# Attention paced by the projections and moved further ahead, the last two heads turned by the tensor engine, and one weight load held back, in a fused attention and MLP block

## The chip, the cores and the metric

The kernel runs on one core of a Trainium2 chip. The metric is the time of one execution on the device, in microseconds (us). A difference counts as faster or slower when it is over 2% and clear of the noise.

TensorE is the matrix engine (PE in the profile), VectorE is DVE, ScalarE is ACT, GpSimd is POOL, and SyncE is SP. The last one only issues DMA transfers here. Below, to turn a matrix is to transpose it, and SBUF is the core's own memory.

## The reference, cut to what matters

```python
# x: (1, 2048, 1024); Wq, Wk, Wv: (1024, 32, 128); Wo: (32, 128, 1024)
# attention in 64 segments of 32 tokens, each with 8 memory tokens in front
def attention(x, mem0, Wq, Wk, Wv, Wo, seg_len):
    for s in range(n_seg):
        h = concat([mem, x[segment s]])
        q, k, v = h @ Wq, h @ Wk, h @ Wv              # 32 heads
        p = softmax(where(mask, q @ k.T * scale, -1e9))
        o = sum over heads of (p @ v) @ Wo
        mem = o[:, :8]; outs.append(o[:, 8:])
...
x = x + ga * attention(layernorm(x) * (1 + ca) + sa, ...)
x = x + gb * mixer_mlp(layernorm(x) * (1 + cb) + sb)  # first product: @ w1
```

The kernel guesses the memory tokens, checks the guess at the end, and so treats all segments at once: 22 tiles of about 99 rows for each head. Most of the projections are computed by a fast matrix product, with seven block products in place of eight; its matmuls are 480 columns wide, and a last part of 199 columns is multiplied in the ordinary way.

## The kernel before: the parts that matter

Three stages matter: the **projections** (Q, K and V of a pair of heads, with the attention of the pair before woven in), the **handover**, and the **Wo blocks** (four blocks of 512 tokens, each over all 32 heads). Then comes the stage that reads `w1s`. The Wo tile (n2, hc) is half n2 of the columns of Wo for group hc of eight heads. In the code below an empty list and the flip of the memory rows, which goes by a small DMA transpose `MT<-O`, are left out.

```python
def attention():                       # the attention as lists of small units, one list a pair
    per_hp = {}; waiting = []
    for h in range(H):
        lst = per_hp.setdefault(h // 2, [])
        for g in range(5):
            lst.append(lambda h=h, g=g: scores(h, g))
            while waiting and waiting[0][0] <= 5 * h + g - 1:
                lst.append(waiting.pop(0)[1])
            for j in range(8):
                if VG[j][-1] // 5 == g:
                    waiting.append((5 * h + g, lambda h=h, j=j: outs(h, j)))
                    if j == 7:
                        waiting.append((5 * h + g, lambda h=h: flip(h)))      # O -> OT by DMA transpose
                        waiting.append((5 * h + g + 3, lambda h=h: keep(h)))  # OT -> OTx_d in memory
                        if h % 2 and h + 2 < H:
                            waiting.append((5 * h + g + 2, lambda h=h: to_v(h + 2)))  # VT -> V by DMA
    per_hp["end"] = [u for _, u in waiting]
...
for hp in range(NHP - 1):              # projections of pair hp + 1, attention of pair hp
    fill = P_units(hp + 1)
    ...
    interleave(att[hp], fill)          # an attention unit, then its share of the projection units
...                                    # --- handover ---
W0, W0_load = W_units(0)               # Wo block 0, as [n2][hc][tt]
for j in range(1, 3):
    W0_load(0, j, nc.gpsimd)           # Wo tile (0, j), 1 MB, into one of 4 wstream buffers
    load_ot(j, nc.gpsimd)              # OTc j: the turned outputs of 8 heads, 1 MB, from OTx_d
for t, src in RW:                      # four rows, broadcast: 1.5 MB
    nc.gpsimd.dma_start(t[:], src.partition_broadcast(P))
load_wo2(NHP - 2)
interleave(att[NHP - 1], M_units(NHP - 3) + [lambda: load_wo2(NHP - 1)] + W0[0][0] + W0[0][1] + M_units(NHP - 2))
for u in att["end"] + W0[0][2]:
    u()
for j in range(3, 6):
    load_ot(j)
...
for us in W0[1][0:3] + W0[0][3:] + W0[1][3:]:   # heads 24..31 (hc = 3) last
    for u in us:
        u()
...
for blk in range(1, 4):
    ...
    else:                              # before block 3, in the program's order
        nc.sync.dma_start(w1s[:], B_w1.rearrange("(k p) n -> p k n", p=P))   # 2 MB
```

The order of each engine's instructions is set by a scheduler when the kernel is built: work that is ready early is moved ahead. So `w1s`, written before block 3, is issued in block 0. The `SyncE` queue is then worked off in order.

## Time and profile before

Median 1517.26 us of four runs (1515.22 to 1517.58); the profiled execution spans 1517.1 us.

I read the length of each stage from the timeline of TensorE. The projections run from the first fast-product matmul (at 122 us) to the end of the last one over 199 columns; the handover ends with the first matmul of Wo block 1, so it holds the last two heads and block 0; the blocks end with the first matmul that reads `w1s`.

| stage | us before | what TensorE waits for in it |
|---|---|---|
| start | 122.1 | not touched |
| projections with attention | 661.1 | some 12 us in all |
| handover, block 0 | 90.2 | 24.4 us, and half clock |
| Wo blocks 1 to 3 | 169.6 | under 1 us, but half clock at its start |
| rest | 474.0 | not touched |

TensorE's waits by line and releaser, before. The columns are the us in total, how often, and the longest:

```profile
PE ps_o L713 <- DMA V<-VT: 15.0, 2, 13.6
...
PE acc L845 <- DMA wstream<-in_A_Wo_dram: 7.2, 1, 7.2
...
PE acc L607 <- ACT snap L575: 3.8, 14, 0.5
PE acc L845 <- DMA OTc<-OTx_d: 3.6, 2, 1.8
PE acc L328 <- DVE KT L579: 3.3, 2, 1.7
...
PE acc L607 <- DVE VT L579: 1.6, 3, 1.1
```

L713 is the outputs of the attention, L845 the Wo blocks, L607 and L328 the projections. The first, second and fourth lines belong to the handover, apart from 1.5 us for V at the very start. The timeline of TensorE shows where they sit; each line has start, length, instructions, and in brackets the idle time before it and what ended it:

```profile
796.03 1.90 PE L845 MATMUL acc<-wstream,OTc 128*128 128x512 bf16 x8 [1.83 <-DMA OTc<-OTx_d]
...
815.64 0.86 PE L713 MATMUL ps_o<-V,E 104*104 104x129 bf16 x6 [13.56 <-DMA V<-VT]
...
850.96 2.76 PE L845 MATMUL acc<-wstream,OTc 128*128 128x512 bf16 x12 [1.77 <-DMA OTc<-OTx_d]
...
873.45 31.89 PE L845 MATMUL acc<-wstream,OTc 128*128 128x512 bf16 x134 [7.24 <-DMA wstream<-in_A_Wo_dram]
```

Why V of head 31 came so late is seen in the timeline of the SyncE queue, with start and time spent at issuing. The lines between are left out:

```profile
785.21 16.14 SPq L728 DMA_TRANSPOSE OT<-O  x1
...
803.66 5.33 SPq L650 DMA_TRANSPOSE V<-VT  x1
...
824.32 9.13 SPq L728 DMA_TRANSPOSE OT<-O  x1
...
849.82 0.84 SPq L978 DMA_DIRECT2D w1s<-in_B_w_dram  x1
```

Issuing the transpose of head 29 alone held the queue for 16 us, while 6.5 MB of the handover's loads, issued from 783.3 to 788.5 us, were in flight. V stood behind it. The last view is of stretches of five microseconds, with each engine's busy time, then the granted TensorE clock (1.00 is full), the busy share of the DMA engines, and GB/s:

```profile
810.00:815.00 5.00, 0.00 (x0) 0.00 (x0) 0.00 (x0) 0.00 (x0) 0.00 (x0) 0.50 1.08 237
815.00:820.00 5.00, 4.36 (x17) 2.32 (x18) 1.50 (x5) 0.88 (x3) 0.00 (x0) 0.50 0.98 236
...
870.00:875.00 5.00, 1.55 (x4) 0.59 (x5) 4.90 (x10) 1.93 (x5) 0.59 (x2) 0.50 1.07 372
875.00:880.00 5.00, 5.00 (x15) 1.89 (x14) 0.61 (x3) 0.00 (x0) 0.00 (x0) 0.59 1.09 383
```

After the two long waits TensorE worked at half clock for a while, and the DMA engines were full throughout.

### The profile page before, as it was taken

The page shows a single profiled execution, that of the slowest core. Times are in us where ns is not written, and L with a number is a line of the kernel's source. Part 1 is how long each engine was busy: PE and PEld are TensorE (multiplying, and loading weights), DVE is VectorE, ACT ScalarE, POOL GpSimd, SP SyncE. Part 2 cuts the span into 40 slices and gives each one's busy share as a digit, 9 for nine tenths or more (in the row PEclk, how much of TensorE's full clock was granted, in tenths as well). Part 3 has the DMA queues.
Part 4 walks back from the last instruction along what each step waited for, and adds up shares of the span by engine and source line. Part 5 has one row for each costly group of instructions (what it writes and reads, how often), then busy time and mean ns, then how long its engine had stood idle before and what let it go on. Part 6 is the DMA issues. An engine that isn't in the chain of part 4 may idle for free.

```text
span 1517.1 us, 24283 instructions
## 1 busy us (share of the span) xinstructions
PE 1429.2 (94%) x9074; PEld 760.1 (50%) x9074; DVE 921.4 (61%) x1961; ACT 668.2 (44%) x1403; POOL 356.1 (23%) x490
## 2 busy tenths in 40 slices
PE   5699999999999999999996799999997999999998
PEld 3365555556555655555653344444443444444443
DVE  5827777677676676766751343363287657675684
ACT  2715666665656665665650020122533661046400
POOL 7501100000000000000010222122011654535625
PEclk9999999999999999999998999999999999999999
DMA  9577779877778876778689999994299784377812
GB/s 307 193 279 158 154 163 197 169 161 158 152 163 197 169 171 153 154 159 193 131 220 292 323 328 327 290 270 146 64 276 270 231 265 157 100 246 240 281 52 77
DMA packets 406900, 304.81 MB, mean 201 GB/s; under 512 B 203370, under 2 KB 359018, under 8 KB 404850
## 3 DMA queue, kind: packets, MB, share of 16 engines
q1 hardware_dynamic: 367920, 239.39, 61.3%
q0 software_dynamic: 9616, 33.05, 7.3%
q10 hardware_dynamic: 29234, 30.71, 6.6%
q8 instruction: 73, 1.20, 0.3%
q14 instruction: 57, 0.47, 0.1%
HBM read 200.82 MB, written 50.63 MB: 166 GB/s over the span
## 4 chain that ended last, share of the span: by engine, by line
PE 73%; DMA 8%; issue 6%; DVE 5%; ACT 4%; POOL 3%; SPq 1%; ACTq 0%; DVEq 0%; POOLq 0%
PE acc L607 28%; PE bank_b L1202 6%; PE acc L845 6%; PE bank_b L1151 6%; PE acc L995 4%; PE acc L328 4%; PE bank_d L1151 3%; PE bank_d L1202 2%; PE bank_e L1202 2%; PE ps_o L713 2%; PE ps_s L698 2%; PE acc L318 2%; PE acc L1078 2%; PE bank_e L1151 1%; DVE ln_st L104 1%
## 5 line engine op out<-in xcount | busy, mean ns | idle before, releaser
L845 PE MATMUL acc<-wstream,OTc 128*128 128x512 bf16 x960 | 214.7, 385 | 11.3 <-DMA wstream<-in_A_Wo_dram 7.2
L607 PEld LDWEIGHTS <-T 128*128 128x128 f16 x1408 | 131.1, 97 | 123.2 <-issue 7.4
L575 ACT COPY snap<-acc 128x480 f32<-128x480 f32 x264 | 146.6, 564 | 101.9 <-PE acc L607 91.3
L607 PE MATMUL acc<-hs,T 128*128 128x480 f16 x704 | 158.5, 365 | 4.9 <-ACT snap L575 3.8
L607 PE MATMUL acc<-hh,T 128*128 128x480 bf16 (+1 forms) x704 | 162.3, 366 | 0.5 <-DVE VT L579 0.5
L845 PEld LDWEIGHTS <-OTc 128*128 128x128 bf16 x960 | 94.4, 99 | 124.8 <-DMA wstream<-in_A_Wo_dram 7.4
L740 POOL DMA_DIRECT2D OTx_d<-OT x32 | 24.8, 775 | 511.4 <-DMA OT<-O 495.2
L1151 PEld LDWEIGHTS <-ring 128*128 128x128 f16 (+1 forms) x784 | 77.5, 99 | 109.5 <-issue 17.6
L702 ACT ACTIVATE E<-ps_s 99x495 bf16<-99x495 f32 (+2 forms) x160 | 86.3, 543 | 65.0 <-PE ps_s L698 63.3
L607 PE MATMUL acc<-hh,wq 128*128 128x480 bf16 x464 | 105.3, 366 | 0.0
L579 DVE TENSOR_TENSOR KT<-acc,snap 128x480 bf16<-128x480 f32 x116 | 74.6, 655 | 47.0 <-PE acc L607 45.4
L720 DVE TENSOR_TENSOR O<-ps_o,rin_all 99x384 bf16<-99x384 f32 (+1 forms) x192 | 96.6, 510 | 3.8
L713 PE MATMUL ps_o<-V,E 99*99 99x129 bf16 (+2 forms) x704 | 81.1, 222 | 16.0 <-DMA V<-VT 15.0
L713 PEld LDWEIGHTS <-E 99*99 99x99 bf16 (+2 forms) x704 | 69.2, 127 | 53.2 <-issue 20.4
L1202 PEld LDWEIGHTS <-hq 128*128 128x128 bf16 (+1 forms) x560 | 54.9, 98 | 66.0
L1116 ACT COPY snap<-bank_b 128x512 f32<-128x512 f32 x72 | 40.6, 583 | 102.0 <-PE bank_b L1202 58.3
L715 DVE RECIPROCAL rin_all<-ps_o 99x3 f32<-99x3 f32 (+2 forms) x256 | 43.3, 173 | 68.8 <-PE ps_o L713 67.9
L718 ACT ACTIVATE O<-ps_o,rin_all 99x128 bf16<-99x128 f32 x192 | 56.6, 368 | 61.8 <-DVE rin_all L715 61.7
L1021 DVE TENSOR_TENSOR ring<-ring 128x1024 f16<-128x1024 bf16 (+1 forms) x64 | 75.5, 1200 | 5.5 <-PE bank_b L1202 5.1
L704 DVE TENSOR_TENSOR E<-E,maskB 99x495 bf16<-99x495 bf16 (+1 forms) x128 | 47.3, 377 | 51.5 <-ACT E L702 51.2
L110 POOL TENSOR_TENSOR ln_rstd<-ln_ve,mhalf 128x1 f32<-128x1 f32 x64 | 35.2, 550 | 173.7 <-DVE ln_ve L108 129.8
L938 ACT ACTIVATE u<-x,ln_nmr,ln_rstd 128x1024 bf16<-128x1024 f32 x16 | 19.7, 1232 | 123.9 <-DVE ln_nmr L937 75.0
(223 smaller groups left out, 2569.9 us busy)
## 6 DMA issues: line engine op xcount, KB each, us to landing
wstream<-in_A_Wo_dram SPq DMA_DIRECT2D x29, 1024.0 KB, 9.0
OTx_d<-OT POOLq DMA_DIRECT2D x32, 512.0 KB, 7.5
wstream<-in_B_w_dram SPq DMA_DIRECT2D x28, 512.0 KB, 4.4
ring<-in_B_w_dram SPq DMA_DIRECT2D x28, 512.0 KB, 5.5
ring<-in_B_w_dram SPq DMA_DIRECT2D x8, 1792.0 KB, 10.0
OTc<-OTx_d SPq DMA_DIRECT2D x13, 1024.0 KB, 8.3
wq<-in_A_Wq_dram SPq DMA_DIRECT2D x16, 512.0 KB, 7.6
wk<-in_A_Wk_dram SPq DMA_DIRECT2D x16, 512.0 KB, 8.5
```

Of the source, the lines that this page charges most:

```text
L328: nc.tensor.matmul(acc[:, 0:CONV], lhsT=W[:, kt, hl * P:(hl + 1) * P], rhs=hh[:, kt, MAIN:MAIN + CONV], start=(kt == 0), stop=(kt == KT - 1))
L575: nc.scalar.copy(t[:], st[q][bank][:, 0:CH])
L579: nc.vector.tensor_tensor(view(d, i), chunks(st[q][bank]), chunks(st[q][s_]), ALU.add)
L607: nc.tensor.matmul(acc[:, 0:CH], lhsT=B[:, k, :], rhs=A[:, k, :], start=(j in (1, 2, 5) and k == 0), stop=(k == 3), skip_group_check=True)
L702: nc.scalar.activation(E[:rows, 0:o], ps[:rows, 0:o], ACT.Exp, scale=DH ** -0.5)
L713: nc.tensor.matmul(ps[:rows, i, :], lhsT=state["e", h, t // 5][:k, col0(t) - col0(t // 5 * 5):col0(t) - col0(t // 5 * 5) + rows], rhs=V[:k ...
L720: nc.vector.tensor_tensor(O[:rows, ts[0]:ts[0] + n, :], ps[:rows, 0:n, 0:DH], rin[:, :, None].to_broadcast([rows, n, DH]), ALU.mult)
L845: nc.tensor.matmul(accs[tt][:], lhsT=ot[hl // 4][:, hl % 4, tt * P:(tt + 1) * P], rhs=woc[hl // 4][:, hl % 4, :], start=(h == 0), stop=(h ...
L995: nc.tensor.matmul(acc[:], lhsT=w1s[:, kt, ct * P:(ct + 1) * P], rhs=zT[:, kt, b * 512:(b + 1) * 512], start=(kt == 0), stop=(kt == KT - 1))
L1021: return nc.vector.tensor_tensor(dst, a, b, op)
L1151: nc.tensor.matmul(acc[:], lhsT=B[:, k, q * P:(q + 1) * P], rhs=A[:, k, :], start=(start and k == 0), stop=(k == 3), skip_group_check=True)
L1202: nc.tensor.matmul(acc[:], lhsT=L3[:, k, i * P:(i + 1) * P], rhs=R3[:, k, :], start=(start and k == 0), stop=(k == 13), skip_group_check=True)
```

## The change

The intent: let less attention be left at the handover, so that V of head 31 is turned before the DMA engines fill; spare the last two heads (all but their memory rows) the way through DMA transpose, memory and reload; and keep `w1s` out of the way of the Wo tiles. The diff, cut to its core (bookkeeping and assertions left out):

```diff
-                    units += d[:6] + [lambda: to_v(2 * hp)] + d[6:] if s == 2 else d
+                    units += d[:1] + [lambda: to_v(2 * hp)] + d[1:] if s == 2 else d
...
+        def turn(h, c):                        # 8 tiles of head h by the tensor engine
+            O, ts = Os[h % 2], list(range(8 * c, min(8 * c + 8, NT)))
+            ...
+            pt = psS.tile([P, 8, P], BF16, name="ps_s")
+            for i, t in enumerate(ts):
+                nc.tensor.transpose(pt[:, i, 0:96], O[0:96, t, :], ident[0:96, 0:96])
+            dst, src = state["ot", h][:, ts[0]:ts[-1] + 1, :], pt[:, 0:len(ts), 0:96]
+            if c == 1:
+                nc.vector.tensor_copy(dst, src)
+            else:
+                nc.scalar.copy(dst, src)
+            if c == 2:                         # the memory rows still go by DMA
+                nc.sync.dma_start_transpose(state["mt", h][:], O[96:112, :, :].rearrange("p t c -> p (t c)"))
...
-                            if j == 7:
+                            if h >= H - 2:
+                                if j in (3, 6):
+                                    waiting.append((5 * h + g, lambda h=h, j=j: turn(h, j // 3 - 1)))
+                                elif j == 7:
+                                    waiting.append((5 * h + g + 1, lambda h=h, j=j: turn(h, 2)))
+                                    waiting.append((5 * h + g + 1, lambda h=h: keep(h)))
+                            elif j == 7:
...
+        done, ahead = 0, len(att) - int(len(att) * 1.55 / H)     # att is one list now
...
-            interleave(att[hp], fill)
+            for i, u in enumerate(fill):
+                u()
+                upto = int(ahead * (hp + (i + 1) / len(fill)) / (NHP - 1))
+                for a in att[done:upto]:
+                    a()
+                done = upto
...
-        RW = ((ga_b, rows_d[0]), (gb_b, rows_d[1]), (sb_b, rows16_d[0]), (cb1_b, rows16_d[1]))
+        RW = ((ga_b, rows_d[0]), (sb_b, rows16_d[0]), (cb1_b, rows16_d[1]))
...
-            eng.dma_start(ot[:], OTx_d[j // 4, j % 4])
+            n = 6 if j == 3 else 8
+            eng.dma_start(ot[:, 0:n], OTx_d[j // 4, j % 4, :, 0:n])
...
-        interleave(att[NHP - 1], M_units(NHP - 3) + [lambda: load_wo2(NHP - 1)] + W0[0][0] + W0[0][1] + M_units(NHP - 2))
-        for u in att["end"] + W0[0][2]:
+        interleave(att[done:], M_units(NHP - 3) + [lambda: load_wo2(NHP - 1)] + W0[0][0] + W0[0][1])
+        load_ot(3)
+        for u in W0[0][2]:
             u()
-        for j in range(3, 6):
+        for h in range(H - 2, H):
+            nc.vector.tensor_copy(ots[3][1][:, h % 8 - 4, :], last_ot[h][:].rearrange("p t c -> p (t c)")[:, 64:576])
+        for u in M_units(NHP - 2):
+            u()
+        for j in range(4, 6):
             load_ot(j)
...
-                nc.sync.dma_start(w1s[:], B_w1.rearrange("(k p) n -> p k n", p=P))
+                ld = nc.sync.dma_start(w1s[:], B_w1.rearrange("(k p) n -> p k n", p=P))
+                tc.add_manual_dep(ld.ins, marks[1].ins.name, ...Sync...)   # wait for the end of block 1
+                nc.gpsimd.dma_start(gb_b[:], rows_d[1].partition_broadcast(P))
```

Below, "the weave" is the pacing by the projection units, the shift ahead and the earlier V; "the turn" is heads 30 and 31 on the tensor engine and from SBUF; "the hold" is the wait of `w1s`.

## The prediction

> **What bounds it now.** TensorE is busy 94% of 1517.1 us (busy table). From 120 to 783 us, projections with attention woven in, its waits sum to about 12 us (list of waits); from 881 us to the end of the Wo blocks at 1043 us, to under 1 us. The hole is at the handover between them, where TensorE's timeline shows four waits:
> - 1.83 us at 794: the first loads of OTc (issued 784.4, landed 796.0).
> - 13.56 us at 802: head 31's outputs wait for V. The transpose OT<-O of head 29 held the in-order SyncE queue 16.1 us; V's transpose followed only at 803.7.
> - 1.77 us at 849: OTc with heads 30, 31, after OT<-O (11.5 us), its store (9.5) and the reload (5.0), in the chain of waits.
> - 7.24 us at 866: a Wo tile, beside w1s (2 MB, issued 849.8, 13.2 us to land).
>
> Sum 24.4 us. After two of them the clock was granted at 0.5 (windows of 5 us from 810 and 870): 16 matmuls took about 430 ns each instead of 216, and 134 took 31.9 us instead of 28.9: 6 to 7 us more. The Trainium skill ("TensorE: Matmul & The Clock Gate", Part 1) has half clock after an idle window of about 3.4 us; the trace agrees. So the hole is worth 31 us.
>
> **What the change does.**
> - 0.45 head of attention (about 1 us of TensorE) moves into the projections, so V(31) and OT(29) get ahead of the handover loads: the 13.6 us should vanish.
> - Two DMA transposes (6.7 and 9.1 us of queue time) become 44 tensor transposes, estimated at 45 to 50 ns from the score matmuls of like size (5 in 0.24 us): 2 us; six evictions and two copies, about 5 us, on ScalarE and VectorE, which have room (13 and 31% busy from 783 to 874). The chain OT, store, reload leaves the path: 1.8 us.
> - w1s waits for the end of block 1: the 7.2 us should go; later there is room (DMA share 0.45 and 0.01 from 1020 to 1040). gb_b is issued right after head 30's store, so hardly deferred.
> - V of the even head turned earlier: nothing to gain before the handover (1.5 us in all).
>
> **What stays.** From 785 to 905 us the DMA engines are near full (share about 1, 240 to 420 GB/s). In the new order about 10 MB are queued up to and with the Wo tile for (1,0): at 350 GB/s, an estimate from those windows, 28 us, as long as the tensor work ahead of it. I expect 5 to 9 us of new waits for wstream and OTc there, and about 1 us of half clock. Handover to block 1's first matmul falls from 90 us to about 69.
>
> Sum: -24.4 waits, -6.5 clock, +2 transposes, +7 waits, +1 clock: -21 us.
>
> **Predicted: 1496 us, 8 in 10 between 1489 and 1505.** Faster by over 2%: 0.06; within 2%: 0.93; slower: 0.01. Even the full hole is hardly 2%.
>
> **Right if:** ps_o <- V is gone from TensorE's waits; no wait for OTc with heads 30, 31; waits for wstream and OTc sum to 4 to 10 us, none above 5; clock at 1.0 nearly throughout 790 to 900; the stage that reads w1s starts near 1021 without a wait.
>
> **Wrong if:** DMA is the real limit of the handover and waits only change names (then near 1508); the new weave adds waits on ScalarE or VectorE over 660 us (1% is 6.6 us); the transposes, sharing the two score banks, stall TensorE; or, on the good side, the loads keep up (then 1489).

## The result, and the profile after

Median 1497.7 us of four runs (1496.59 to 1498.23), ratio 0.9873 with a 95% interval of 0.9856 to 0.9890. A ratio is the mean time of one kernel's fast runs over that of the other's of the same rounds, so it is not quite the ratio of the medians quoted. The change is 19.6 us faster by the medians, within 2%. The profiled execution spans 1496.1 us, 21.0 less than before's.

| stage | before | after | difference |
|---|---|---|---|
| start | 122.1 | 122.5 | +0.4 |
| projections with attention | 661.1 | 656.9 | -4.2 |
| handover, block 0 | 90.2 | 76.1 | -14.1 |
| Wo blocks 1 to 3 | 169.6 | 166.9 | -2.7 |
| rest | 474.0 | 473.7 | -0.3 |

The waits of TensorE after (L877 is the Wo blocks now, L716 the outputs, L608 the projections):

```profile
PE acc L877 <- DMA OTc<-OTx_d: 4.8, 1, 4.8
PE ps_o L716 <- DMA V<-VT: 4.3, 4, 1.5
PE acc L877 <- DMA wstream<-in_A_Wo_dram: 4.0, 1, 4.0
...
PE acc L608 <- ACT snap L576: 0.6, 3, 0.2
...
PE acc L608 <- DVE VT L580: 0.3, 1, 0.3
```

The 13.6 us wait for V and the 7.2 us wait at block 1 are gone. In the projections the waits for ScalarE's and VectorE's evictions are nearly gone too, while V has three more short waits. Two waits of the handover are new, as its timeline of TensorE shows, the only two of it above 0.2 us:

```profile
796.55 3.59 PE L877 MATMUL acc<-wstream,OTc 128*128 128x512 bf16 x8 [4.83 <-DMA OTc<-OTx_d]
...
818.09 8.77 PE L877 MATMUL acc<-wstream,pre_o 128*128 128x512 bf16 x32 [4.03 <-DMA wstream<-in_A_Wo_dram]
```

Eight matmuls took 3.59 us where eight at full clock take 1.89, and 32 took 8.77 us where others take 7.07. With the two groups after the first of them that is about 4.3 us lost to half clock in the handover, which the stretches of five microseconds show too:

```profile
795.00:800.00 5.00, 3.45 (x9) 1.31 (x10) 0.00 (x0) 0.00 (x0) 1.78 (x5) 0.50 0.98 369
800.00:805.00 5.00, 5.00 (x32) 2.71 (x31) 1.84 (x6) 0.88 (x3) 0.00 (x0) 0.83 1.03 387
...
820.00:825.00 5.00, 5.00 (x20) 2.09 (x19) 1.25 (x3) 0.00 (x0) 0.49 (x3) 0.78 1.03 265
```

The SyncE queue after, around the end of the projections at 779.5 us:

```profile
766.69 2.54 SPq L731 DMA_TRANSPOSE OT<-O  x1
...
770.96 3.39 SPq L652 DMA_TRANSPOSE V<-VT  x1
...
779.81 0.82 SPq L843 DMA_DIRECT2D OTc<-OTx_d  x2
...
785.37 0.58 SPq L843 DMA_DIRECT2D OTc<-OTx_d  x1
785.99 0.51 SPq L860 DMA_DIRECT2D wstream<-in_A_Wo_dram  x1
786.54 10.29 SPq L843 DMA_DIRECT2D OTc<-OTx_d  x1
...
804.52 11.24 SPq L761 DMA_TRANSPOSE MT<-O  x1
```

The transpose of head 29 and V of head 31 now go out in 2.5 and 3.4 us, before the loads of the handover. But OTc for heads 24 to 29 and for block 1, not needed for 40 us and more, stands ahead of the Wo tile issued at 785.99, which landed only 32.1 us later. The last line is what the turn left to DMA: the small transpose of head 31's memory rows held the queue 11.2 us.

### The profile page after: what moved, and what is told of

Its sections match the earlier page's. It is cut to its first block, busy times and chain, and to the rows that moved or that the text cites. A ratio compares the mean times of both kernels' runs of the same rounds, so it can differ in the third digit from the quotient of the medians.

```text
span 1496.1 us, 24409 instructions
## 1 busy us (share of the span) xinstructions
PE 1428.8 (95%) x9118; PEld 761.0 (51%) x9118; DVE 931.4 (62%) x1965; ACT 666.3 (45%) x1407; POOL 360.3 (24%) x490
## 4 chain that ended last, share of the span: by engine, by line
PE 79%; DMA 6%; DVE 5%; issue 4%; ACT 3%; POOL 3%; ACTq 0%; SPq 0%; DVEq 0%; POOLq 0%
PE acc L608 31%; PE acc L877 7%; PE bank_b L1241 6%; PE bank_b L1190 6%; PE acc L1034 4%; PE acc L1117 3%; PE acc L328 3%; PE bank_d L1190 3%; PE bank_d L1241 2%; PE bank_e L1241 2%; PE ps_o L716 2%; DMA wstream<-in_A_Wo_dram 2%; PE ps_s L700 2%; PE acc L318 2%; DMA V<-VT 2%
## 5 line engine op out<-in xcount | busy, mean ns | idle before, releaser
L877 PE MATMUL acc<-wstream,OTc 128*128 128x512 bf16 x960 | 211.1, 382 | 5.3 <-DMA OTc<-OTx_d 4.8
L608 PEld LDWEIGHTS <-T 128*128 128x128 f16 x1408 | 130.8, 98 | 118.9 <-issue 1.7
L608 PE MATMUL acc<-hh,T 128*128 128x480 bf16 (+1 forms) x704 | 163.1, 366 | 0.3 <-DVE VT L580 0.3
L608 PE MATMUL acc<-hs,T 128*128 128x480 f16 x704 | 157.1, 366 | 0.6 <-ACT snap L576 0.6
L877 PEld LDWEIGHTS <-OTc 128*128 128x128 bf16 x960 | 94.0, 98 | 118.4 <-DMA OTc<-OTx_d 5.0
L608 PE MATMUL acc<-hh,wq 128*128 128x480 bf16 x464 | 103.9, 366 | 0.0
L1060 DVE TENSOR_TENSOR ring<-ring 128x1024 f16<-128x1024 bf16 (+1 forms) x64 | 85.7, 1359 | 5.8 <-PE bank_b L1241 5.4
L716 PEld LDWEIGHTS <-E 99*99 99x99 bf16 (+2 forms) x704 | 67.7, 126 | 39.4 <-issue 5.4
L716 PE MATMUL ps_o<-V,E 99*99 99x129 bf16 (+2 forms) x704 | 80.5, 221 | 5.9 <-DMA V<-VT 4.3
L580 DVE TENSOR_TENSOR VT<-acc,snap 128x480 bf16<-128x480 f32 x90 | 58.0, 651 | 25.0 <-PE acc L608 21.0
## 6 DMA issues: line engine op xcount, KB each, us to landing
ring<-in_B_w_dram SPq DMA_DIRECT2D x8, 1792.0 KB, 10.2
```

The costliest lines, as they stand in the source:

```text
L580: nc.vector.tensor_tensor(view(d, i), chunks(st[q][bank]), chunks(st[q][s_]), ALU.add)
L608: nc.tensor.matmul(acc[:, 0:CH], lhsT=B[:, k, :], rhs=A[:, k, :], start=(j in (1, 2, 5) and k == 0), stop=(k == 3), skip_group_check=True)
L716: nc.tensor.matmul(ps[:rows, i, :], lhsT=state["e", h, t // 5][:k, col0(t) - col0(t // 5 * 5):col0(t) - col0(t // 5 * 5) + rows], rhs=V[:k ...
L877: nc.tensor.matmul(accs[tt][:], lhsT=ot[hl // 4][:, hl % 4, tt * P:(tt + 1) * P], rhs=woc[hl // 4][:, hl % 4, :], start=(h == 0), stop=(h ...
L1060: return nc.vector.tensor_tensor(dst, a, b, op)
```

## The experiments

Each kernel computed a correct result. The stages of each are from its own profile, in us:

| kernel | projections | handover | Wo blocks | median, ratio to before |
|---|---|---|---|---|
| before | 661.1 | 90.2 | 169.6 | 1512 to 1521 on the other chips |
| the change | 656.9 | 76.1 | 166.9 | 1497.7, 0.9873 |
| e1_w1s: the hold alone | 660.7 | 81.8 | 170.5 | 1510.75, 0.9962 |
| e2_weave: the weave alone | 652.4 | 80.4 | 167.3 | 1497.75, 0.9885 |
| e3_turn: the turn alone | 663.4 | 81.9 | 166.8 | 1504.73, 0.9921 |
| e6_pace: the pacing alone | 656.9 | 90.5 | 169.7 | 1512.41, 0.9985 |
| after_again: the change again | 657.3 | 76.0 | 167.2 | 1496.65, 0.9873 |
| e5_nohold: the change less the hold | 657.2 | 76.3 | 166.8 | 1497.44, 0.9880 |
| e9_left175: the change, less far ahead | 652.1 | 77.9 | 166.9 | 1496.60, 0.9875 |
| e4_loads: the change, loads reordered | 657.2 | 72.2 | 166.9 | 1492.92, 0.9841 |
| e7_order: more of that | 657.1 | 64.3 | 171.0 | 1486.98, 0.9811 |
| e8_best: all loads in order of need | 652.3 | 65.4 | 166.9 | 1481.88, 0.9780 |

The intervals of the ratios are about 0.002 to each side (e6: 0.003). The profiled executions of e3 and e9 are the longest of their kernels' runs, 4.4 and 5.9 us above the median. Single runs of before scattered from 1512 to 1521 us on these chips, more than in the first runs, so differences of 3 us in the medians are not to be built on; the stages of the profiles repeat better, as the change and its repetition show.

### e1_w1s: the hold alone

The kernel before, with this:

```diff
-                nc.sync.dma_start(w1s[:], ...)
+                ld = nc.sync.dma_start(w1s[:], ...)
+                tc.add_manual_dep(ld.ins, marks[1].ins.name, ...Sync...)
```

> The kernel before, with one thing of the change: the load of w1s waits for the end of Wo block 1. Theory (each of the four handover waits has its own cause): the 7.2 us wait for a Wo tile at block 1's start and the 3 us of half clock after it go, nothing else moves: about 10 us less, near 1507. Rival (the DMA engines are the limit of the whole handover and of the Wo blocks, so the 2 MB must be paid somewhere): the wait comes back at another Wo tile or at w1s itself, under 4 us less, 1513 or more.

Measured: 5.7 us less by the medians; in the profile the handover is 8.4 us shorter. The wait at the start of block 1 and its half clock are gone. But the timeline shows a new wait for a Wo tile, in block 2, after `w1s` had been issued at 927 us:

```profile
949.94 50.40 PE L846 MATMUL acc<-wstream,OTc 128*128 128x512 bf16 x226 [2.67 <-DMA wstream<-in_A_Wo_dram]
```

So both theories hold in part: the wait goes from where it was, and about a third of it comes back where the 2 MB are moved to.

### e2_weave: the weave alone

The kernel before with one list of units, the loop of the change, `1.55`, and `d[:1]`; flips, `w1s` and the rows as before. Its core:

```diff
-            interleave(att[hp], fill)
+            for i, u in enumerate(fill):
+                u()
+                upto = int(ahead * (hp + (i + 1) / len(fill)) / (NHP - 1))
+                for a in att[done:upto]: a()
+                done = upto
```

> The kernel before, with the attention moved: paced by the projection units, 0.45 head further ahead, V of the even head turned earlier; heads 30 and 31 still turned by DMA, w1s not held back. Theory: the waits in the projections fall as in the changed kernel (about 4 us), the 13.6 us wait for V and its half clock go, and the new waits for OTc and the Wo tile of (1,0) appear (about 9 us with 4 us of clock); the 7.2 us wait stays: about 10 us less, near 1507. Rival (the four projection microseconds came by chance or from elsewhere in the change, and the DMA transposes of heads 30 and 31 now stand in the way): at most 4 us less, 1513 or more.

Measured: 18.7 us less by the medians, about twice what was expected, and as much as the whole change within the error. The projections are 8.7 us shorter. The handover is 9.8 us shorter, with these waits among its five:

```profile
789.59 3.59 PE L847 MATMUL acc<-wstream,OTc 128*128 128x512 bf16 x8 [4.10 <-DMA OTc<-OTx_d]
...
837.92 4.96 PE L847 MATMUL acc<-wstream,OTc 128*128 128x512 bf16 x12 [8.47 <-DMA wstream<-in_A_Wo_dram]
```

There is no 7.2 us wait at block 1 although `w1s` is not held back; but an 8.5 us wait for another Wo tile, with half clock from 832.2 to 842.4 us, has come in block 0. It is a matter of the queue: the load of OTc with heads 30 and 31 has to wait for their store, and the next Wo tiles are issued behind it.

```profile
817.93 0.37 SPq L980 DMA_DIRECT2D w1s<-in_B_w_dram  x1
828.68 0.34 SPq L814 DMA_DIRECT2D OTc<-OTx_d  x1
829.12 2.48 SPq L830 DMA_DIRECT2D wstream<-in_A_Wo_dram  x2
```

The turn takes that wait away: neither the change nor e5 below, which has the turn but not the hold, has a wait there. (`w1s` shared the DMA engines with these loads until it landed at 832.3 us; how much it added was not measured.)

### e3_turn: the turn alone

The kernel before with `turn`, the load of 6 of 8 heads and the two copies from SBUF, as in the diff above; attention and `w1s` as before.

> The kernel before, with heads 30 and 31 turned by the tensor engine and used from SBUF, attention and w1s as before. Theory: head 31 waits for V as before (13 us), only the 1.8 us wait for OTc with heads 30 and 31 goes, and 2 us of tensor work come: within 3 us of before. Rival (the two DMA transposes were the weight on the DMA engines, so without them all the later loads land earlier): 7 us less or more, the Wo tile's 7.2 us wait gone too.

Measured: 11.8 us less by the medians. The rival's forecast came true: the wait for V of head 31 is there in full, yet no wait for a Wo tile or OTc is left in the whole profile, although `w1s` is not held back (it is issued at 837.7 us, even earlier than the 849.8 before). The rival's reason, the weight of the two transposes on the DMA engines, is not shown apart from another: before, they also held the SyncE queue for 6.8 and 9.1 us, with the Wo tiles and OTc behind them. This is the first of its list of waits:

```profile
PE ps_o L714 <- DMA V<-VT: 16.4, 2, 14.9
```

The handover is 8.3 us shorter and the blocks 2.8, the latter because block 1 starts at full clock. In the projections this one profile has a single 4.8 us wait for VectorE, with half clock after it, where the others have at most 1.8 us; I have no cause for it, and this execution is longer than the others of its kernel by about as much.

e1, e2 and e3 together: the hold, the weave and the turn are worth 5.7, 18.7 and 11.8 us by themselves, 36 in sum, and 19.6 together. In all three the same 7.2 us wait at block 1 and the half clock after it are gone, so that they cannot be added; but e1 has 2.7 us of wait in block 2 instead, and e2 the 8.5 us in block 0.

### after_again and e5_nohold: is the hold needed in the change?

e5_nohold is the change without the `add_manual_dep` line for `w1s`. The change itself was run beside it.

> The changed kernel, unaltered, as a measure for the other runs on this chip: 19 to 20 us less than before, as in its first runs.

> The changed kernel without the hold on w1s, so that its 2 MB are issued at the end of the handover again. What e1 and e3 showed (either the hold or the missing DMA transposes removed the 7.2 us wait at block 1) makes one theory: the wait had several sufficient remedies, the hold is spare in the changed kernel, under 3 us are lost. The other (each remedy pays for its own part): a Wo tile at the end of block 0 or the start of block 1 waits 4 to 8 us and half clock follows, 5 to 10 us more than the changed kernel.

Measured: 1497.44 us without the hold and 1496.65 with it, on the same chip. The three stages agree within about 0.4 us. The waits of e5 are 5.6 us where the change has 4.0, and 4.0 where it has 4.8:

```profile
PE acc L877 <- DMA wstream<-in_A_Wo_dram: 5.6, 1, 5.6
...
PE acc L877 <- DMA OTc<-OTx_d: 4.0, 1, 4.0
```

The hold is spare in the change. What it did alone, the other parts do too. (`gb_b`, moved along with it, stays moved in e5; it was not tried by itself.)

### e6_pace: where the projections gained

The kernel before with the new loop, but with two heads left for the handover and `to_v` at `d[:6]`:

```diff
+        done, ahead = 0, state["cut"]        # the units before scores(30, 0)
-            interleave(att[hp], fill)
+            for i, u in enumerate(fill): ... # as in the change
```

> The kernel before, with only the pacing changed: attention units follow the projection units, two heads left for the handover as before, V of the even head where it was. Theory (the projections gained because pacing spreads the attention, not because of the 0.45 head or the earlier V): the waits for ACT snap (3.8 us), DVE KT (3.3) and DVE VT (1.6) vanish, the projections end 6 to 9 us sooner, the handover stays at about 90 us: near 1510. Rival (the earlier V or the shift did it): the projections keep their 661 us, within 3 us of before.

Measured: the median is 3.2 us lower, but the interval (0.9953 to 1.0017) includes 1, so no gain in time is shown. In the profile the projections take 656.9 us, 4.2 less than before, and the handover 90.5 as before. The waits the loop was to remove are smaller by 5.7 us (8.7 before, 3.0 here), and one other has come:

```profile
PE ps_o L713 <- DMA V<-VT: 13.2, 2, 11.9
...
PE ps_o L713 <- ACT O L718: 2.7, 1, 2.7
...
PE acc L328 <- DVE KT L579: 1.8, 2, 1.2
...
PE acc L607 <- ACT snap L575: 1.2, 3, 0.8
```

The gain is less than the 6 to 9 us expected, and by the profiles it is part of the 8.7 us of e2. Whether the rest comes with the shift or the earlier V was not tried, and perhaps neither is needed: the wait of 2.7 us, at 134.5 us, is followed by half clock until 137.3, together about 4.1 us, nearly all that e6 lacks against e2. One profile does not tell whether it belongs to the pacing or to this execution. The first line also shows that pacing alone does nothing for V of head 31: that takes the shift.

### e9_left175: how far ahead

Why are the projections of the change 4.5 us longer than those of e2, with the same 1.55 in the code? The number cuts a list of units, not of heads. The last two heads have 15 units each in e2 and 17 in the change, where three turns stand for one flip. So e2 leaves 23 of 495 units, about 1.53 heads, and the change 24 of 499, about 1.41. The attention then runs up to V, which cannot be turned before it is projected.

```diff
-        done, ahead = 0, len(att) - int(len(att) * 1.55 / H)
+        done, ahead = 0, len(att) - int(len(att) * 1.75 / H)
```

> The changed kernel with 1.75 heads left for the handover instead of 1.55. In the changed kernel the projections end 4.5 us later than in e2, and 3 of that are waits for V of heads 28 to 30, three attention units earlier in the stream. Theory (the attention runs up to the turning of V): those waits go, the projections take 653 to 654 us instead of 657, the handover stays at 76 +- 2: near 1494. Rival (the shift is worth its full length, less of it brings the wait for V of head 31 back): handover 80 or more, 1499 or more.

Measured: the projections take 652.1 us, as the theory said. But the time is 1496.60, ratio 0.9875, no better than the change. The handover has grown by 1.8 us, and most of the rest is lost outside the stages in question: the profiled execution (1502.48 us) is the longest of its four runs, with one 7.5 us wait in the MLP, at 1138 us, that no other kernel has. The other three lie between 1494.9 and 1497.4. Whether the 5 us reach the time in this kernel stays open. The waits show why the handover gave some back:

```profile
PE acc L877 <- DMA wstream<-in_A_Wo_dram: 10.1, 1, 10.1
...
PE ps_o L716 <- DMA V<-VT: 1.4, 1, 1.4
```

TensorE reaches the Wo tile of (1,0) sooner and waits for it longer.

### e4_loads: the order of the loads

The change, with the two Wo tiles loaded first and a chain of issue order (no wait) behind them:

```diff
+        for j in range(2):
+            W0_load(1, j)
         load_wo2(NHP - 2)
         interleave(att[done:], ...)
...
+            if 3 <= j <= 6:                  # in load_ot: behind the load issued before
+                tc.add_manual_dep(ins.ins, order[-1].ins.name, ...NoSync...)
```

> The changed kernel, with only the order of the SyncE queue's loads changed at the handover: the Wo tiles (1,0) and (1,1) are issued ahead of OTc for heads 24 and up and for block 1. Theory (the new waits of 4.8 and 4.0 us come from the order of the loads: 2 to 3 MB that nobody needs for 40 us share the DMA engines with the first loads and stand ahead of the Wo tile): both waits and the 4.6 us of half clock after them go, 10 to 13 us less than the changed kernel, near 1486. Rival (the DMA engines are simply full there, the order does not matter): the waits only change names, within 4 us of the changed kernel's 1497.7.

Measured: 1492.92 us, about 5 less than the change. The handover is 3.9 us shorter. The wait for OTc is gone, so it was one of order. The wait for the Wo tile has shrunk from 4.0 to 3.3 us, and another of 2.7 has come at tile (1,2), which stood behind OTc for block 1:

```profile
PE acc L882 <- DMA wstream<-in_A_Wo_dram: 6.0, 2, 3.3
```

Neither theory fits whole: the handover got a third (3.9 us) of the 11.8 us that e7 will reach, and the rest needed more of the traffic moved.

### e7_order: more traffic moved

e4 with these:

```diff
-        for t, src in RW: ...                # before the handover
+        for t, src in RW:                    # behind the store of head 31
+            ins = nc.gpsimd.dma_start(t[:], src.partition_broadcast(P))
+            tc.add_manual_dep(ins.ins, state["store"].ins.name, ...NoSync...)
         load_ot(3)
+        W0_load(1, 2)                        # ahead of OTc for block 1
...
+                tc.add_manual_dep(<gb_b>, marks[1]..., Sync)
```

> The changed kernel with the loads of the handover in the order of need: Wo tiles (1,0), (1,1) and (1,2) ahead of OTc for block 1, and the three row loads (1 MB) after the last store of the attention, gb_b after block 1. e4 left waits of 3.3 and 2.7 us. Theory (what is left is 2 to 3 MB of early traffic ahead of the Wo tiles): both waits and the half clock go, the handover takes 63 to 66 us instead of 72, near 1486. Rival (the handover is at the limit of the DMA engines): it stays near 1492.

Measured: 1486.98 us, ratio 0.9811 with an interval of 0.9794 to 0.9827, so that faster by over 2% is neither shown nor excluded; the handover takes 64.3 us, as the theory said. But the Wo blocks take 171.0 instead of 167, and the timeline shows why:

```profile
828.22 2.75 PE L882 MATMUL acc<-wstream,OTc 128*128 128x512 bf16 x12 [1.38 <-DMA wstream<-in_A_Wo_dram]
...
929.80 84.74 PE L882 MATMUL acc<-wstream,OTc 128*128 128x512 bf16 x384 [2.92 <-DMA wstream<-in_A_Wo_dram]
```

The second wait lies in block 2, after `w1s` and `gb_b` were let go: the hold now ends too early.

### e8_best: all loads in the order of need

e7 with `1.75` as in e9, and with both holds until the end of block 2:

```diff
-                tc.add_manual_dep(..., marks[1].ins.name, ...Sync...)    # w1s and gb_b
+                tc.add_manual_dep(..., marks[2].ins.name, ...Sync...)
```

> e7 with 1.75 heads left and with w1s and gb_b held until the end of Wo block 2 instead of block 1. e7 had the handover at 64 us but waited 2.9 us in block 2 for a Wo tile behind w1s and gb_b, and its Wo blocks took 171 us instead of 167. Theory: the blocks fall back to 167 us, the projections to 654, the handover stays: near 1480. Rival (the blocks as a whole are at the limit of the DMA engines, an earlier start only moves the wait): the wait turns up at another Wo tile or at w1s, 1485 or more.

Measured: 1481.88 us (1480.35 to 1483.86), ratio 0.9780 with an interval of 0.9762 to 0.9798: faster than before by over 2%, and the fastest of all. Projections, handover and blocks are 652.3, 65.4 and 166.9 us. These are all the waits of the handover and the blocks above 0.2 us:

```profile
795.57 7.08 PE L882 MATMUL acc<-wstream,OTc 128*128 128x512 bf16 x32 [0.36 <-DMA OTc<-OTx_d]
...
825.27 2.75 PE L882 MATMUL acc<-wstream,OTc 128*128 128x512 bf16 x12 [1.90 <-DMA wstream<-in_A_Wo_dram]
...
929.52 77.86 PE L882 MATMUL acc<-wstream,OTc 128*128 128x512 bf16 x360 [0.49 <-DVE x L884]
```

The clock stays at 1.00 throughout these stages, with the DMA engines as full as ever:

```profile
795.00:805.00 10.00, 9.64 (x45) 4.33 (x45) 0.00 (x0) 0.00 (x0) 0.20 (x1) 1.00 1.11 324
805.00:815.00 10.00, 10.00 (x48) 4.51 (x46) 3.34 (x10) 0.00 (x0) 2.39 (x6) 1.00 1.00 341
815.00:825.00 10.00, 8.37 (x39) 3.72 (x38) 0.00 (x0) 0.00 (x0) 0.00 (x0) 1.00 1.05 380
```

So full DMA engines were not the limit of the handover; what they carried first was.

## Why the prediction was right, and where it was not

- **The time.** 1496 was predicted and 1497.7 measured, inside the range. The sum came out at -21 and the profiles differ by 21.0, but two terms were off in opposite ways (the half clock and the projections, below). That they nearly cancelled is luck; the mechanism of the handover was right for the most part.
- **The wait for V of head 31** (13.6 us) went, as said. e6 shows that it took more than the pacing, which alone left 11.9 us of it: the shift, as the earlier V concerns the even heads alone. The prediction's own test, `ps_o <- V` gone from the list, was met for this wait only: 4.3 us of short ones are left before the handover.
- **The wait for OTc with heads 30 and 31** (1.8 us) went, as said, and more hung on it: in e2, without the turn, that load blocks the queue and costs 8.5 us at a Wo tile.
- **The wait at block 1** (7.2 us) went, but the reason given, the hold on `w1s`, was wrong as a reason for this kernel. The hold alone suffices for it (e1, with 2.7 us back in block 2), and so does the turn alone (e3); with the weave alone it is gone too, but 8.5 us have come before it (e2). Without the hold nothing is lost (e5).
- **New waits for `wstream` and OTc of 5 to 9 us, none above 5.** Measured 8.8 us, 4.8 and 4.0. The prediction ascribed them to full DMA engines. e4, e7 and e8 show that they came from the order of the loads.
- **Half clock: -6.5 and +1.** This term was mis-sized. The new waits brought a loss of about 4.3 us by it, not 1. "Clock at 1.0 nearly throughout" did not hold: adding up the stretches of five microseconds, the clock was at half for 6.8 us at the first new wait (its last part included) and 3.4 at the second.
- **The handover: 69 predicted, 76.1 measured.** Besides the clock, 2.8 of the 6.5 us counted there lie behind the first matmul of block 1, as 134 matmuls took 31.9 instead of about 29 us. They are the blocks' gain of 2.7. The 44 transposes cost about 2 us, as said (43 ns each), and TensorE waits for no score bank in the list.
- **The projections: nothing predicted, 4.2 us gained.** The prediction feared that the new weave might add waits and gave the earlier V nothing to gain. In fact the waits for ScalarE and VectorE fell from 8.7 us (3.8, 3.3 and 1.6) to about 1 us, against 2.8 us of new waits for V. This offset the mis-sized clock.
- **"0.45 head".** By the count of units it was about 0.59, which brought the new waits for V (e9).
- **The stage that reads `w1s`** was to start near 1021 us without a wait; it started at 1022.5 without one.
- **Nothing over 2%.** Right for the change, since about four tenths of the hole (8.8 us of waits and 4.3 us lost to half clock, of 31) was dug again. e8 shows that the hole and the projections together hold more than 2%.

## What to carry to other kernels

Where DMA engines are full at a change of stage, first look at what stands ahead of the load that is waited for, or moves beside it: moving some 5 MB that nobody needed for tens of microseconds behind it (3.75 MB of OTc, 1 MB of rows, 0.5 MB of `gb_b`) took the handover from 76 to about 65 us. A wait that several parts of a change remove must be counted once; undo each part by itself before crediting it. And count a wait of some 3 us or more with the half clock that follows it.

## What the Trainium skill lacked or had wrong

- "TensorE: Matmul & The Clock Gate", Part 1, says that the clock halves after about one idle window of 3.4 us, and that the window is not tied to the kernel's own times. The runs agree: half clock lasted 13.6 and 10.2 us before and 6.8 and 3.4 after, multiples of it. What the page lacks in its advice under "Why this matters for your kernels" (no gaps above about 3 us) is that the edge is blurred downwards: waits of 2.7 us (e1, block 2; e4) and of 2.9 us (e7, block 2; granted clock 0.83 over the next 10 us) were each followed by half clock, 3.4 us of it in all, while one of 2.8 us in e6 and waits of 1.8 us before and 1.9 us in e8 cost none.
- The same page, Part 4, gives about 275 to 390 ns for a 128x128 transpose on TensorE and no rate for a stream of them (for matmuls its Part 2 has one). Here eight transposes of 96x96 in a row took 0.34 us from start to the start of what followed (789.22 to 789.56 us), 43 ns each. The page's duration would have made the 44 of them cost 12 us or more; they cost 2.
- "DMA: Bandwidth & Descriptors", Issuing engines are not separate DMA queues, calls the time to initiate a DMA usually small against the DMA. The runs show that it can be large with many loads in flight: issuing one transpose held the SyncE queue 16.1 us in the kernel before against 2.5 in the change, where it went out ahead of them, and a plain load of OTc held it 10.3 us in the change. What stands behind is late by that much. Full DMA engines alone do not decide it: the transpose `MT<-O` of head 31 took 11.2 us to issue in the change and 1.4 in e8, both at a DMA share of about 1. The section's other statement, that transfers of all queues interleave on the same engines, fits the landing of 32.1 us for a 1 MB tile behind and beside the other loads.
- The same page, Latency and other measured facts, gives 261 GB/s for a DMA transpose that is not contiguous. It gives no size of transfer. Here OT<-O (22 x 96 x 128 elements of two bytes, 0.54 MB, from SBUF to SBUF, contiguous in each partition) landed a median 5.2 us after its issue in the kernel before, about 104 GB/s with the issue counted and other transfers beside it.
